# Two attention and gated-MLP layers on one core: block sums by adding transfers in DRAM, and three moves on VectorE and GpSimd

## The chip, the core and the metric

The kernel runs on one core of a Trainium2 chip. A core has TensorE (PE in the profile; its weight loads are PEld), VectorE (DVE), ScalarE (ACT), GpSimd (POOL) and SyncE (SP, which here only issues transfers), 16 DMA engines, an on-chip memory SBUF, and PSUM, eight banks of 128 x 512 float32 that matmuls write into. The metric is the time of one execution on the device in microseconds (us).

## What is computed

Two layers, each a linear-attention block A and then a gated mixer B, both with a residual. All is float32. S = 2048 rows, D = 512, 32 heads of 16, F = 1792 (halves of 896).

```python
x = x + A(layernorm(x));  x = x + B(layernorm(x))      # twice, same weights

def A(x):                       # linear attention
    q, k, v = heads(x @ wqkv)
    phi = lambda t: where(t > 0, t + 1, exp(t)) + 1e-6
    kv = sum_s phi(k)[s] * v[s];  z = sum_s phi(k)[s]
    return (phi(q) @ kv / (phi(q) . z + 1e-6)) @ wo

def B(x):                       # gated mixer
    z = gelu(x @ w_in); z1 = z[:, :896]; z2 = layernorm(z[:, 896:])
    g = w_sp @ z2 + b_sp        # w_sp is 2048 x 2048: it mixes rows
    return (z1 * g) @ w_out
```

## The kernel before

**Split operands.** Every large product is made from two float32r parts of each operand: a high part (a ScalarE copy, `high`, L119) and a low part, the rest (a VectorE subtraction, `low`, L122; for some weights GpSimd's, L127). Three matmuls add up to one product (`mm3`, L133 to L135; `acc`, L902 to L904).

**Order.** The order of instructions on every engine is written out by hand: each engine runs its own in the order of the program and waits on semaphores for the others. SP issues all transfers of before, in program order. Buffers come from rotating lists: 22 pages of 128 x 512 (`pages`, pg), six `quads` (qd) of 2048 columns, four `bigs` (bg), and the eight PSUM banks (`banks`). A buffer's next user waits for its last one.

**P1** (`P1.run`), steps s = 1 to 17, one tile of 128 rows each. A step turns the normalised tile so that its features lie on partitions, splits it (`T_high`, `T_low`), multiplies with the key weights (K), and, up to step ND = 10, with the query weights (Q); the last six query products are put off (`late`, `late_phi`). `Gmm` adds phi(k) transposed times x, two steps behind, in four banks that stay taken. The turning goes through DRAM and a block transpose on VectorE (L260); the first three tiles of the first layer are turned by PE instead. `phi` is ReLU and Exp on ScalarE (L327, L328) and one VectorE operation (L329). `K_split` makes the key's high part (ScalarE, L340) and low part (VectorE, L341), and GpSimd adds the keys up for z (`zacc`, L346). The mixer's second weight `win2` is loaded and split piece by piece in steps 7 to 13 (`side`), loaded a step ahead.

**transition and P2.** `transition` makes the block-diagonal product of the attention, while late query products fill PE. `P2.run`, steps s = 1 to 18: `c` (attention output, added to x by VectorE at L614, then `stats`, L196 to L203, which ends on GpSimd), `b_high` and `b_low` (the next query tile's parts), `a`/`a2` (denominators: GpSimd L561, VectorE L573 to L582), `d` (turned mixer input), `e` (second half of the mixer's input product), `f` (first half). In steps 1 to 4 the remaining late query products (`late`) and their phi (`late_phi`) are woven in.

**P4.** The mixer's 2048 x 2048 product by a fast scheme of seven passes (P2, P1, P6, P7, P4, P5, P3) over 2 x 2 blocks of w_sp. Three passes read blocks of w_sp itself, four read sums of blocks. Then the gates (GpSimd, L929) and the output product `o`.

**Sums.** Class `Sums` makes the four block sums once, in the first layer: a21 + a22 (m = 1), m1 + a11 (m = 2), a21 + a11 (m = 3), m2 + a12 (m = 4), for eight k and two j. A `tick` loads blocks of 128 x 512 into pages, adds them on GpSimd (L782) and stores the sums to DRAM in the next tick (L777). There are 32 ticks with work: four in P1's steps 2 to 5 (on borrowed `bigs`, class `Sheets`), then one in each of P2's steps from 6 on, and P4's first ones. P4 reads each sum tile with one transfer of 512 KB (L831). The second layer reads the same tiles.

Of the kernel before, what the change touches and what calls it, by code (L numbers as in the profile page):

```python
# [52 lines left out]
class Sheets:  # L53


    def __init__(self, slots, n):
        self.slots = slots
        self.tiles = [slots.get([P, NF, 512]) for _ in range(n)]
        self.free_list = deque(t[:, f, :] for t in self.tiles for f in range(NF))

    def get(self, shape):
        return self.free_list.popleft()

    def put(self, *sheets):
        self.free_list.extend(sheets)

    def close(self):
        self.slots.put(*self.tiles)


@with_exitstack
def mixer_kernel(ctx: ExitStack, tc: tile.TileContext, x_in, wqkv, wo_d, win1_d, win2_d, wsp_d, bsp_d, wout_d,
# [40 lines left out]
    def load(ap, slots=pages):  # L113
        t = slots.get(PAGE)
        nc.sync.dma_start(t, ap)
        return t

# [106 lines left out]
    class Turn:  # L224
# [3 lines left out]
        def __init__(self, name, by_pe, always=False):  # L228
            self.name, self.by_pe, self.always = name, by_pe, always
            self.held, self.d, self.raw = {}, {}, {}  # L230
# [20 lines left out]
        def get(self, i):  # L251
# [7 lines left out]
            y = pages.get([P, 4, P])  # L259
            nc.vector.transpose(y.rearrange("p c (t m) -> p m c t", m=4), r.rearrange("p (m c j) -> p m c j", m=4, c=4))  # L260
            pages.put(r)
            return y, pages


    class P1:
        def __init__(self, L):
# [59 lines left out]
        def phi(self, b, r):  # L326
            nc.scalar.activation(r, b, AF.Relu, scale=-1.0)  # L327
            nc.scalar.activation(r, r, AF.Exp, scale=-1.0)  # L328
            nc.vector.scalar_tensor_tensor(r, b, 0.0, r, op0=OP.max, op1=OP.add)  # L329
            banks.put(b)  # L330
# [6 lines left out]
        def K_split(self, i):  # L337
# [3 lines left out]
            nc.vector.scalar_tensor_tensor(l, r, PHI_EPS, h.bitcast(F32), op0=OP.add, op1=OP.subtract)  # L341
            self.pk[i] = (h, l)
            if i == 0:
                self.zacc = r
            else:
                nc.gpsimd.tensor_tensor(self.zacc, self.zacc, r, op=OP.add)  # L346
                pages.put(r)
# [18 lines left out]
        def late_phi(self):  # L366
            if self.later:
                self.Q_phi(self.later.popleft())
# [60 lines left out]
        def run(self, sums):  # L429
            side = deque([self.win2] * NF)  # L430
            ND = NT - DEFER
            for s in range(1, NT + 2):
# [41 lines left out]
                if s > 6 and side:  # L474
                    side.popleft().piece()
                if s > 5 and side:
                    side[0].fetch()


    def transition(p1, p2):  # L480
# [58 lines left out]
        p1.late_phi()  # L539


    class P2:
# [152 lines left out]
        def run(self, sums):  # L695
            w1 = self.win1
            for s in range(1, NT + 3):
                self.loadx(s + 1)
                self.qturn.load(s + 1)
                if s in self.qturn.by_pe:  # L700
                    self.c(s - 1)
                    self.b_high(s)
                    self.c2(s - 1)
                    self.b_low(s)
# [6 lines left out]
                    self.p1.late_phi()  # L711
# [37 lines left out]
                if s > 5:  # L749
                    sums.tick()  # L750
# [6 lines left out]
    class Sums:  # L757

        def __init__(self):
            self.s = {(m, k): dram.tile([P, 2, 512], F32, name=f"s{m}_{k}") for m in range(1, 5) for k in range(HT)}
            self.todo = deque((k, j, h) for k in range(HT) for j in range(2) for h in range(2))
            self.ahead = deque(self.todo)
            self.raw, self.made, self.done = {}, [], []
            self.slots = pages

        def fetch(self):
            if self.ahead:
                k, j, h = self.ahead.popleft()  # L770
                at = ((j, k), (j, k + HT), (2 + j, k)) if h == 0 else ((2 + j, k + HT),)
                self.raw.setdefault((k, j), []).extend(load(wsp_d[n, s], self.slots) for n, s in at)

        def store(self):

            for m, k, j, t in self.made:
                nc.sync.dma_start(self.s[m, k][:, j, :], t)  # L777
            self.slots.put(*self.done)
            self.made, self.done = [], []

        def add(self, m, k, j, t, a, b):
            nc.gpsimd.tensor_tensor(t, a, b, op=OP.add)  # L782
            self.made.append((m, k, j, t))

        def tick(self, ahead=True):
            self.store()
            if not self.todo:
                return
            if not self.raw:
                self.fetch()  # L790
            if ahead or self.todo[0][2] == 0:
                self.fetch()
            k, j, h = self.todo.popleft()
            if h == 0:
                a21, a22, a11 = self.raw[k, j][:3]
                self.add(1, k, j, a22, a21, a22)
                self.add(3, k, j, a21, a21, a11)
                self.done = [a21]
            else:
                _, a22, a11, a12 = self.raw.pop((k, j))  # L800
                self.add(2, k, j, a11, a22, a11)
                self.add(4, k, j, a12, a11, a12)
                self.done = [a22, a11, a12]


    class P4:
# [15 lines left out]
        def fetch(self, g):  # L822
# [7 lines left out]
            else:  # L830
                nc.sync.dma_start(t, self.sums.s[{"P6": 2, "P7": 3, "P5": 1, "P3": 4}[p], k])  # L831
# [172 lines left out]
        def run(self, nxt):  # L1004
# [10 lines left out]
            for g in range(n):  # L1015
# [9 lines left out]
                if g < 16:  # L1025
                    self.sums.tick()
# [88 lines left out]
```

## Time and profile before

| | |
|---|---|
| median of 3 runs | 1404.9 us (1404.71 to 1405.46) |
| the profiled execution | 1404.73 us, of which its span is 1402.9 us |
| PE busy | 1389.6 us, 99% of the span |
| VectorE, ScalarE, GpSimd busy | 886.4, 561.0, 405.6 us |
| DMA | 225.69 MB in 142263 packets, mean 161 GB/s |
| HBM read and written | 156.63 and 67.90 MB |

The span is the time from the first to the last instruction that the profiler recorded; the profiled execution's own time is 1.8 us longer. "Busy" is the time in which an engine runs an instruction; issuing a transfer isn't counted. In rows with an arrow, `out<-in` names the tile written and those read; `[0.65 <-DVE pg L341]` is idle time of the engine ahead of this instruction and what ended it. A row of the waits gives the total, the number and the longest in us. PE's matmuls overlap in the pipeline, so their starts, not their lengths, tell the pace.

### The profile page before, as it was taken

Reading aid. Unit: us, or ns where it says so; the run is one execution under the profiler, and the core shown is the slowest. Engines: PE = TensorE matmul, PEld = TensorE weight load, DVE = VectorE, ACT = ScalarE, POOL = GpSimd, SP = SyncE. Lnnn points to the kernel's source line nnn. Section 1 sums busy time; section 2 is a strip of 40 time slices with the busy share of each in tenths; the row PEclk is TensorE's granted clock in tenths of the full one; section 3 lists DMA queues with packets and bytes.
Section 4 is the critical chain, followed back from the end, with each engine's and each line's share of the span. In section 5 each row is a group of like instructions: output and inputs, shape, how many; then the busy total and the mean of one; then the engine's idle time right before and its main releaser. Section 6 shows DMA issues by size and latency. Waiting matters only on the chain.

```text
span 1402.9 us, 17320 instructions
## 1 busy us (share of the span) xinstructions
PE 1389.6 (99%) x6230; PEld 1156.7 (82%) x6230; DVE 886.4 (63%) x1251; ACT 561.0 (40%) x847; POOL 405.6 (29%) x490
## 2 busy tenths in 40 slices
PE   9999999999999999999999999999999999999998
PEld 7877788888888888888788778888888888888887
DVE  7786777752577666573577867766415466665632
ACT  5564534434323332341356645444333233333420
POOL 4644345544365002040023434432100030022300
PEclk9999999999999999999999999999999999999999
DMA  5842267876897433443635413555334344334432
GB/s 176 270 142 62 73 192 237 271 228 207 305 326 248 134 120 135 173 158 120 210 101 184 129 46 99 179 179 162 114 116 158 104 165 134 133 117 167 155 110 94
DMA packets 142263, 225.69 MB, mean 161 GB/s; under 512 B 11744, under 2 KB 50400, under 8 KB 142176
## 3 DMA queue, kind: packets, MB, share of 16 engines
q1 hardware_dynamic: 142176, 224.57, 48.6%
q8 instruction: 49, 0.80, 0.2%
q14 instruction: 38, 0.31, 0.1%
HBM read 156.63 MB, written 67.90 MB: 160 GB/s over the span
## 4 chain that ended last, share of the span: by engine, by line
PE 87%; DVE 6%; ACT 4%; issue 1%; DMA 1%; POOL 0%; SPq 0%; DVEq 0%; ACTq 0%; POOLq 0%
PE bank L135 15%; PE bank L134 15%; PE bank L133 15%; PE bank L902 13%; PE bank L904 13%; PE bank L903 13%; DVE pg L260 1%; DVE pg L341 1%; DVE pg L329 1%; ACT pg L328 1%; DMA pg<-in_win_dram 1%; ACT pg L327 1%; PE bank L515 1%; PE bank L526 0%; PE bank L221 0%
## 5 line engine op out<-in xcount | busy, mean ns | idle before, releaser
L902 PE MATMUL bank<-qd,pg 128*128 128x512 f32 x800 | 311.2, 389 | 0.0
L904 PE MATMUL bank<-qd,pg 128*128 128x512 f32 x800 | 311.2, 389 | 0.0
L903 PE MATMUL bank<-qd,pg 128*128 128x512 f32 x800 | 311.2, 389 | 0.0
L841 DVE TENSOR_TENSOR qd<-qd,qd 128x1024 fp32r<-128x1024 f32 x112 | 151.8, 1355 | 178.7 <-ACT qd L840 174.2
L840 ACT ACTIVATE qd<-qd 128x1024 fp32r<-128x1024 f32 x112 | 118.5, 1058 | 215.7 <-PE bank L904 199.0
L929 POOL TENSOR_TENSOR bg<-bg,pg 128x512 f32<-128x512 f32 x56 | 85.5, 1564 | 409.7 <-DVE bg L956 195.5
L904 PEld LDWEIGHTS bank<-qd,pg 128*128 128x128 f32 x800 | 150.2, 188 | 31.3
L903 PEld LDWEIGHTS bank<-qd,pg 128*128 128x128 f32 x800 | 150.2, 188 | 31.2
L902 PEld LDWEIGHTS bank<-qd,pg 128*128 128x128 f32 x800 | 150.1, 188 | 31.1
L135 PE MATMUL bank<-qd,pg 128*128 128x512 f32 x384 | 150.7, 392 | 2.5 <-DVE pg L122 2.5
L200 POOL TENSOR_SCALAR rs<-mv 128x1 f32<-128x1 f32 x96 | 36.4, 379 | 384.4 <-DVE mv L198 377.2
L209 ACT ACTIVATE pg<-pg,nb,rs 128x512 f32<-128x512 f32 x63 | 51.1, 811 | 181.6 <-POOL nb L203 175.5
L133 PE MATMUL bank<-qd,pg 128*128 128x512 f32 x288 | 112.4, 390 | 0.0
L134 PE MATMUL bank<-qd,pg 128*128 128x512 f32 x288 | 112.3, 390 | 0.0
L782 POOL TENSOR_TENSOR pg<-pg,pg 128x512 f32<-128x512 f32 x56 | 81.5, 1456 | 47.7 <-DMA pg<-in_wsp_dram 41.8
L133 PE MATMUL bank<-bg,qd 128*128 128x448 f32 x256 | 94.1, 368 | 0.0
L135 PE MATMUL bank<-bg,qd 128*128 128x448 f32 x256 | 93.7, 366 | 0.1
L134 PE MATMUL bank<-bg,qd 128*128 128x448 f32 x256 | 93.6, 366 | 0.0
L135 PEld LDWEIGHTS bank<-qd,pg 128*128 128x128 f32 x384 | 72.0, 188 | 20.8 <-DVE pg L122 6.0
L135 PE MATMUL bank<-wo,qd 128*128 128x512 f32 x224 | 87.3, 390 | 0.8 <-DVE qd L122 0.8
L133 PE MATMUL bank<-wo,qd 128*128 128x512 f32 x224 | 87.3, 390 | 0.7 <-ACT qd L119 0.7
L135 PE MATMUL bank<-qd,bg 128*128 128x512 f32 x224 | 87.4, 390 | 0.0
(121 smaller groups left out, 2571.7 us busy)
## 6 DMA issues: line engine op xcount, KB each, us to landing
qd<-s SPq DMA_DIRECT2D x64, 512.0 KB, 3.4
qd<-in_wsp_dram SPq DMA_DIRECT2D x48, 512.0 KB, 3.8
pg<-x SPq DMA_DIRECT2D x64, 256.0 KB, 2.9
z<-pg SPq DMA_DIRECT2D x56, 256.0 KB, 2.5
pg<-in_wsp_dram SPq DMA_DIRECT2D x56, 256.0 KB, 5.0
s<-pg SPq DMA_DIRECT2D x56, 256.0 KB, 4.8
pg<-z SPq DMA_DIRECT2D x56, 256.0 KB, 5.4
x<-pg SPq DMA_DIRECT2D x48, 256.0 KB, 2.6
```

The source lines that it names most:

```text
L133: nc.tensor.matmul(out, ah, bh, start=start, stop=False)
L134: nc.tensor.matmul(out, ah, bl, start=False, stop=False)
L135: nc.tensor.matmul(out, al, bh, start=False, stop=stop)
L200: nc.gpsimd.tensor_scalar(rs, mv[:, 1:2], LN_EPS, None, op0=OP.add)
L209: nc.scalar.activation(y, x, AF.Identity, bias=nb, scale=rs)
L782: nc.gpsimd.tensor_tensor(t, a, b, op=OP.add)
L840: nc.scalar.activation(w[:, 0], r, AF.Copy)
L841: nc.vector.tensor_sub(w[:, 1], r, w[:, 0].bitcast(F32))
L902: m(out, h[:, o], w[:, 0, j, :], start=start, stop=False, skip_group_check=True)
L903: m(out, h[:, o], w[:, 1, j, :], start=False, stop=False, skip_group_check=True)
L904: m(out, l[:, o], w[:, 0, j, :], start=False, stop=stop, skip_group_check=True)
L929: nc.gpsimd.tensor_tensor(u, u, z1, op=OP.mult)
```

## The change

Four edits, with no change in what is computed and none in the matmuls.

1. **Block sums.** `Sheets`, the loads, the GpSimd adds and the stores are gone. A sum begins as a copy of a block pair (512 KB) from w_sp to DRAM, issued by SP; a transfer issued by GpSimd adds the second operand onto it in DRAM, in rows of 4096 bytes. Eight groups (j, pair of k) start two ticks apart, each spread over six ticks by `PLAN` ("c1" copies for sum 1, "a1" adds to it). Ticks are in P2's steps from 3 on and P4's first eight steps; 20 have work. P4 reads a sum tile in two halves.
2. **Keys' sum.** GpSimd's add to `zacc` gets a dependency on the key's low part, so that it starts behind it.
3. **Turned tiles.** In P1 of both layers, the block transpose writes a PSUM bank instead of a page.
4. **Late query pass and second weight.** The late phi is cut into its ScalarE part (`phi_a`), which stays, and its VectorE part (`phi_b`), which in P2's first steps goes behind the next step's statistics. In P1, the second weight's loads and splits start three steps sooner.

```diff
+    def behind(ins, other):
+        tc.add_manual_dep(ins.ins, other.ins.name, mybir.DependencyInfo(
+            mybir.DependencyClass.Sync, mybir.DependencyReason.DATA))
...
             r = self.raw.pop(i)
-            y = pages.get([P, 4, P])
+            home = banks if self.inbank else pages
+            y = home.get([P, 4, P])
             nc.vector.transpose(y.rearrange("p c (t m) -> p m c t", m=4), r.rearrange(...))
             pages.put(r)
-            return y, pages
+            return y, home
...
-            self.turn = Turn(f"xt{L}", range(3) if L == 0 else ())
+            self.turn = Turn(f"xt{L}", range(3) if L == 0 else (), False, True)
...
+        def phi_a(self, b, r):
             nc.scalar.activation(r, b, AF.Relu, scale=-1.0)
             nc.scalar.activation(r, r, AF.Exp, scale=-1.0)
+
+        def phi_b(self, b, r):
             nc.vector.scalar_tensor_tensor(r, b, 0.0, r, op0=OP.max, op1=OP.add)
             banks.put(b)
...
-            nc.vector.scalar_tensor_tensor(l, r, PHI_EPS, h.bitcast(F32), op0=OP.add, op1=OP.subtract)
+            last = nc.vector.scalar_tensor_tensor(l, r, PHI_EPS, h.bitcast(F32), op0=OP.add, op1=OP.subtract)
...
-                nc.gpsimd.tensor_tensor(self.zacc, self.zacc, r, op=OP.add)
+                behind(nc.gpsimd.tensor_tensor(self.zacc, self.zacc, r, op=OP.add), last)
...
+        def late_phi_a(self):
             if self.later:
-                self.Q_phi(self.later.popleft())
+                self.half = self.qb, ztag(self.later.popleft(), PAGE, f"q{self.L}")
+                self.phi_a(*self.half)
+
+        def late_phi_b(self):
+            if self.half is not None:
+                self.phi_b(*self.half)
+                self.half = None
...
-                if self.L == 0 and s == 2:
-                    sums.slots = Sheets(bigs, 2)
-                if self.L == 0 and 2 <= s < 6:
-                    sums.tick(s < 5)
-                if self.L == 0 and s == 6:
-                    sums.store()
-                    sums.slots.close()
-                    sums.slots = pages
...
-                if s > 6 and side:
+                if s > 3 and side:
                     side.popleft().piece()
-                if s > 5 and side:
+                if s > 2 and side:
                     side[0].fetch()
...
         p2.a2(2)
-        p1.late_phi()
+        p1.late_phi_a()
...
                     self.c2(s - 1)
+                    self.p1.late_phi_b()
                     self.b_low(s)
...
                     self.a2(s + 2)
-                    self.p1.late_phi()
+                    self.p1.late_phi_a()
                     self.a(s + 3)
...
-                if s > 5:
+                if s > 2:
                     sums.tick()
...
+        GROUPS = [(j, k) for k in range(0, HT, 2) for j in range(2)]
+        PLAN = ("c1", "c3"), ("a1", "c2"), ("a3", "c4"), ("a2",), (), ("a4",)
...
+            self.s = {(m, j, k): dram.tile([2, P, 512], F32, name=f"s{m}_{j}_{k}")
+                      for m in range(1, 5) for j, k in self.GROUPS}
+            n, p = len(self.GROUPS), len(self.PLAN)
+            self.todo = deque([(g, x) for g in range(n) if 0 <= t - 2 * g < p for x in self.PLAN[t - 2 * g]]
+                              for t in range(2 * n + p - 2))
...
+        def tick(self):
             if not self.todo:
                 return
+            for g, (what, m) in self.todo.popleft():
+                j, k = self.GROUPS[g]
+                m = int(m)
+                out = self.s[m, j, k]
+                own, k0 = {1: (j, k), 3: (j, k), 2: (2 + j, k), 4: (2 + j, k + HT)}[m]
+                if what == "c":
+                    nc.sync.dma_start(out, wsp_d[own, k0:k0 + 2])
+                else:
+                    n, s = (j, k + HT) if m == 1 else (2 + j, k)
+                    src = wsp_d[n, s:s + 2] if m % 2 else self.s[m // 2, j, k]
+                    nc.gpsimd.dma_start(out, src, accum_op=OP.add, max_dma_last_dim=4096)
...
-                nc.sync.dma_start(t, self.sums.s[{"P6": 2, "P7": 3, "P5": 1, "P3": 4}[p], k])
+                for j in range(2):
+                    nc.sync.dma_start(t[:, j, :], self.sums.tile({"P6": 2, "P7": 3, "P5": 1, "P3": 4}[p], j, k))
...
-                if g < 16:
+                if g < 8:
                     self.sums.tick()
```

More of the change, by code (lines that the diff above doesn't have):

```diff
@@ L50, in put @@
             self.free_list.append(n)
[L53 to L68, printed above, removed]
 @with_exitstack
@@ L366, in late_phi @@
         def late_phi(self):
+            self.late_phi_a()
+            self.late_phi_b()
+        def late_phi_a(self):
             if self.later:
-                self.Q_phi(self.later.popleft())
+                self.half = self.qb, ztag(self.later.popleft(), PAGE, f"q{self.L}")
[3 more added lines that the diff above has]
+                self.phi_b(*self.half)
+                self.half = None
         def xsplit(self, i):
@@ L757, in mixer_kernel @@
     class Sums:
+        GROUPS = [(j, k) for k in range(0, HT, 2) for j in range(2)]
+        PLAN = ("c1", "c3"), ("a1", "c2"), ("a3", "c4"), ("a2",), (), ("a4",)
         def __init__(self):
[L762 to L786, printed above, removed]
+            self.s = {(m, j, k): dram.tile([2, P, 512], F32, name=f"s{m}_{j}_{k}")
[3 more added lines that the diff above has]
+                              for t in range(2 * n + p - 2))
@@ L787, in tick, with tile @@
+        def tile(self, m, j, k):
+            return self.s[m, j, k - k % 2][k % 2]
+        def tick(self):
             if not self.todo:
                 return
[L789 to L803, printed above, removed]
+            for g, (what, m) in self.todo.popleft():
[9 more added lines that the diff above has]
+                    nc.gpsimd.dma_start(out, src, accum_op=OP.add, max_dma_last_dim=4096)
```

6 lines of the change are left out of this document (4 added, 2 removed).

## The prediction

> **What bounds the kernel now.** I read the page's engine lines first, then who TensorE (PE) waited for, then the PE timeline at those waits, then what the other engines did there.
>
> ```profile
> span 1402.9 us, 17320 instructions
> PE 1389.6 (99%) x6230; PEld 1156.7 (82%) x6230; DVE 886.4 (63%) x1251; ACT 561.0 (40%) x847; POOL 405.6 (29%) x490
> PEclk9999999999999999999999999999999999999999
> ```
>
> PE is busy 99% of the span at full clock. The edits take no matmul away, so only the places where PE stands still can give time: 1402.9 - 1389.6 = 13.3 us by this line. All its waits:
>
> ```profile
> PE bank L134 <- DVE pg L341: 3.2, 5, 0.7
> PE bank L135 <- DVE pg L122: 2.5, 4, 0.7
> PE bank L407 <- DVE pg L402: 2.3, 1, 2.3
> PE bank L135 <- DVE qd L122: 0.8, 1, 0.8
> PE bank L133 <- ACT qd L119: 0.7, 1, 0.7
> ```
>
> The first two rows, nine waits with 5.7 us of idle time, are what the edits touch. L407 is the start, and the last two are split output activations and weights at the seam of the two layers; the diff leaves them alone. A wait costs more than its idle time:
>
> ```profile
> 102.26 0.39 PE L135 MATMUL bank<-qd,pg 128*128 128x512 f32 x1
> 102.49 0.39 PE L133 MATMUL bank<-pg,pg 128*128 128x512 f32 x1
> 103.53 0.50 PE L134 MATMUL bank<-pg,pg 128*128 128x512 f32 x1 [0.65 <-DVE pg L341]
> 103.86 0.39 PE L135 MATMUL bank<-pg,pg 128*128 128x512 f32 x1
> ...
> 121.81 0.39 PE L133 MATMUL bank<-pg,pg 128*128 128x512 f32 x1
> 122.28 0.50 PE L134 MATMUL bank<-pg,pg 128*128 128x512 f32 x1
> ...
> 817.21 0.39 PE L133 MATMUL bank<-pg,pg 128*128 128x512 f32 x1
> 817.72 0.50 PE L134 MATMUL bank<-pg,pg 128*128 128x512 f32 x1
> ```
>
> Matmuls start 0.23 us apart (102.26 to 102.49) though each shows 0.39. At the wait the gap is 1.04, and the next one 0.33: lost are 0.81 + 0.10 = 0.91 us where the row shows 0.65 idle, so 0.26 more. Nine waits: 5.7 + 9 x 0.26 = 8.0 us. Two gaps show no idle time at all (121.81 and 817.21): 0.47 and 0.51 instead of 0.23, with the same 0.10 behind: 0.34 + 0.38 = 0.7 us. **8.7 us in all is what these edits can win.**
>
> **Late key steps (five waits and the two gaps).** From step 11 of P1 on, PE does K and G alone, 24 matmuls x 0.227 = 5.4 us a step, instead of 36 or 8.2 us. VectorE's (DVE's) work doesn't shrink that much:
>
> ```profile
> 97.54:104.00 6.46, 5.81 (x26) 4.35 (x25) 5.87 (x9) 4.13 (x7) 3.10 (x4) 1.00 0.52 162
> 74.20:82.40 8.20, 8.20 (x38) 6.80 (x37) 7.22 (x10) 6.04 (x12) 3.24 (x5) 1.00 0.44 133
> L341 DVE SCALAR_TENSOR_TENSOR pg<-pg,pg x32: 691/1601/1773, 18.9 to 820.1; 128x512 fp32r<-128x512 f32 x32
> L346 POOL TENSOR_TENSOR pg<-pg,pg x30: 1291/1662/1676, 24.1 to 819.5; 128x512 f32<-128x512 f32 x30
> L122 DVE TENSOR_TENSOR bg<-pg,bg 128x512 fp32r<-128x512 f32 x14 | 9.5, 682 | 3.9 <-ACT bg L119 3.8
> ```
>
> The first two rows (columns: length, then PE, weight loads, DVE, ACT, POOL busy) are one late step, cut from one transpose to the next, and one full step. In the late step DVE is busy 5.87 of 6.46 us, more than PE's 5.4: DVE sets the pace and PE waits for the key's low part, L341. Two edits cut there.
> - The keys' sum (POOL, L346) runs beside L341 now, and both are stretched: L341 0.69 at its least, where no sum runs, and 1.60 in the middle; L346 1.29 and 1.66. Put behind L341, it leaves 0.91 us a step to DVE. What it meets next in a late step has one operand in SBUF (transpose, statistics, low part from PSUM), so I take no new stretch there; in full steps it meets the weight's low part, at most 0.91 back, where DVE has 8.20 - 7.22 = 1.0 us to spare.
> - The second weight's seven pieces move from steps 7-13 to 4-10: 0.68 us of DVE leave steps 11-13 and enter full steps. There DVE now has 7.22 with L341 stretched and a piece in it already; steps 4-6 become like 7-10, in which PE doesn't wait. The seven fetches go with them on SP's queue; eight block loads and stores of the first layer leave it there.
>
> The late step becomes 5.87 - 0.91 - 0.68 = 4.3 us of DVE under 5.4 of PE. The chain fits as well: from the end of K through two ACT passes, phi, the key's high and low part, five operations at 0.6 to 0.7 or 3.3 us, against the 5.4 us of G and the next K. I count the five waits and both gaps as gone: 3.2 + 5 x 0.26 + 0.7 = 5.2 us.
>
> **Turned tiles in PSUM.** No row shows DVE writing PSUM. The nearest rows:
>
> ```profile
> L260 DVE STREAM_TRANSPOSE pg<-pg 128x512 f32<-128x512 f32 x75 | 80.7, 1077 | 3.9 <-DMA pg<-yt 3.1 <-DMA pg<-xt 0.5 <-issue 0.2
> L122 DVE TENSOR_TENSOR pg<-pg,pg 128x512 fp32r<-128x512 f32 x71 | 54.6, 770 | 13.1 <-ACT pg L119 12.5
> L122 DVE TENSOR_TENSOR pg<-bank,pg 128x512 fp32r<-128x512 f32 x13 | 8.7, 672 | 0.8 <-ACT pg L119 0.7
> ```
>
> Reading PSUM made the low part 0.10 shorter, so I bound the transpose at -0.1 to +1.08 (twice as long) and take 0, the nearest row. Even doubled it leaves a late step at 5.4, equal to PE. The tile takes one of the four banks that G leaves; K's, Q's and this one rotate, and each is next used about a step after its reader ended, so no wait is added.
>
> **Late query pass (four waits).** At the entry of P2, in both layers:
>
> ```profile
> 149.00 0.39 PE L135 MATMUL bank<-qd,pg 128*128 128x512 f32 x1
> 152.64 0.39 PE L134 MATMUL bank<-qd,pg 128*128 128x512 f32 x1
> 153.73 0.50 PE L135 MATMUL bank<-qd,pg 128*128 128x512 f32 x1 [0.70 <-DVE pg L122]
> 150.74 0.58 ACT L119 ACTIVATE pg<-bank 128x512 fp32r<-128x512 f32 x1
> 150.87 0.69 DVE L329 SCALAR_TENSOR_TENSOR z_q<-bank,z_q 128x512 f32<-128x512 f32 x1 [1.91 <-ACT z_q L328]
> 151.48 0.68 DVE L614 TENSOR_TENSOR pg<-pg,bank 128x512 f32<-128x512 f32 x1
> 152.19 0.69 DVE L196 BATCH_NORM_STATS2 st<-pg 128x6 f32<-128x512 f32 x1
> 152.92 0.18 DVE L198 BATCH_NORM_AGGREGATE mv<-st 128x2 f32<-128x6 f32 x1
> 153.01 0.66 DVE L122 TENSOR_TENSOR pg<-bank,pg 128x512 fp32r<-128x512 f32 x1
> ```
>
> DVE stood 1.91 us for ACT's exponential before the query's L329, with L614 behind it, whose matmul ended at 149.4. After the change L614, statistics and aggregate (1.53 us as spaced here) fill that hole, done at 150.95; L329 goes from there to 151.6, and the low part, whose ACT half ended at 151.32, to 152.3. PE wants it at 152.87: 0.6 us early. What is late next is nothing within the step; the second wait a step on is the same picture. The query's bank stays held half a step longer, while eight banks turn and the second product hasn't begun. Gain 2.5 + 4 x 0.26 = 3.5 us.
>
> **Block sums.** Gone: 64 loads and 64 stores of 256 KB on SP and 64 POOL adds. New: 32 copies of 512 KB in DRAM (SP), 32 adding transfers (POOL), over 20 ticks, 16 in P2's steps and four in P4; the sum tiles are then read in halves, 64 more issues. SP's issues fall by 32 net.
>
> ```profile
> 164.00:360.00 196.00, 195.94 (x910) 169.06 (x909) 123.13 (x193) 82.70 (x134) 91.04 (x134) 1.00 0.67 217
> 860.00:1056.00 196.00, 196.00 (x911) 169.65 (x910) 113.94 (x193) 83.58 (x134) 54.50 (x106) 1.00 0.46 150
> 534.00:535.00 1.00, 1.00 (x6) 0.84 (x5) 0.67 (x1) 0.00 (x0) 0.00 (x0) 1.00 1.12 434
> ...
> 254.13 2.66 POOL L782 TENSOR_TENSOR pg<-pg,pg 128x512 f32<-128x512 f32 x2
> 258.97 0.56 POOL L200 TENSOR_SCALAR rs<-mv 128x1 f32<-128x1 f32 x1 [2.19 <-DVE mv L198]
> ```
>
> P2 of the first layer (with sums) and of the second (without) both take 196 us with PE full: today's sums cost nothing, and taking the adds away wins nothing. The question is what replaces them. *POOL:* two adds (2.66 us a step) end 2.2 us before the next statistics; two transfers a step stay within that 4.9 us if one issue costs up to 2.4. No row has a POOL issue: from 0 to, say, an add's 1.33 each; I take 1.33, hidden. Behind it wait the statistics, then ACT's normalising. *DMA:* a P2 step is 196/16 = 12.25 us. The other traffic is 150 GB/s x 12.25 = 1.84 MB; two copies and two adding transfers a step come on top, 1.05 MB of payload each pair. The adding price is in no row: one pass (like a copy) to three (both reads and the write apart). The rate lies between 150/0.46 = 326 and the busiest microsecond's 434 GB/s. Best: 3.94 MB / 434 = 9.1 us. Worst: 6.04 MB / 326 = 18.5. I take two passes at the busiest rate, as queues would be full: 4.99 / 434 = 11.5 us, 94% of the step, so 0 lost. This is the weakest term.
>
> The Trainium skill ("Collectives: The Full Stack", "The bandwidth ceiling: the fold count and why AG ≠ RS ≠ AR") says that a transfer which adds reads two sources and so runs at half a copy's rate; no run here shows it. By it the sum is that of two passes; with it and the lower rate, 326, a step would take 15.3 us and the kernel 3.05 x 14 - 12 = 31 us more, 1427, which is a case of rival 1 below.
>
> **Sum:** 5.2 + 3.5 = 8.7 us off the profiled execution's 1404.73, 1396.0; the median of before lies 0.2 higher. **Prediction 1396.0 us**; own range 1394.5 to 1398.5.
>
> **Rivals.**
> 1. *DMA saturates in the first layer's P2 (slower).* It decides from 12.25 us of DMA a step: with two passes, below 407 GB/s. At three passes and the middle rate of 380: 6.04/380 = 15.9, 3.6 us too many over about 14 full ticks, 51 us, less about one step (12 us), since by the order of the code a turned tile is used a step after it is made: +39, 1435 us; worst (18.5 - 12.25) x 14 - 12 = +75, 1471. For it: both the price and the mixture are unseen, and 94% leaves little. Against it: today's 0.67 moves PE by nothing. Chance 0.26.
> 2. *The saturation just eats the gain*: 1402 to 1407.5, for example two passes at 365 GB/s: 13.7 us a step, 1.42 x 14 - 12 = +8, 1404 us. For and against it stands the same as in 1. Chance 0.08.
> 3. *The late steps don't do what they are meant to*: the sum stretches another DVE operation, or a transpose into PSUM takes twice as long; then only the entry of P2 gains, 1404.7 - 3.5 = 1401.2. For it: POOL and DVE do meet wherever both read SBUF twice. Against it: 1.1 us to spare a step. Chance 0.12, range 1398.5 to 1402.
>
> **Chances.** Forecast 0.54; 0.2% (2.8 us) is about what a measurement of this kernel can tell from no change, so rival 3 also counts as faster: 0.66 faster, 0.08 same, 0.26 slower. Range 1394.5 to 1412: it leaves out 0.02 below and some 0.18 of rival 1.
>
> **What would show it.** Right: L341 near 0.69 in all steps, no PE wait on L341's and L122's successors near 102-122, 150-161, 804-818 and 848-856, PE idle near 5 us. Wrong: a PE wait between 180 and 400, DMA share of P2 near 1, POOL waiting at its transfers, or late steps still 6.4 us apart.

## The result and the profile after

The changed kernel takes 1438.0 us (median of four runs, 1435.9 to 1442.9) against 1405.2 us (1404.7 to 1405.8) for the kernel before on the same chip: ratio 1.0238 [1.0212, 1.0265], slower by 32.8 us. The profiled execution took 1437.4 us. Forecast were 1396.0 us; rival 1, slower in the first layer's P2, is what happened.

Line numbers below are those of the kernel that the fence comes from: 120 to 122 of the changed kernel are the three matmuls that were 133 to 135, 336 is the key's low part (341 before), 248 the block transpose (260), 97 the helper that issues loads (115), and 885 to 887 P4's matmuls (902 to 904). The page of the changed kernel (span, busy time by engine, granted clock in 40 slices, GpSimd's DMA queue, chain that ended last):

```profile
span 1434.8 us, 17177 instructions
PE 1399.5 (98%) x6230; PEld 1165.0 (81%) x6230; DVE 822.0 (57%) x1251; ACT 562.1 (39%) x847; POOL 322.7 (22%) x458
PEclk9999998999999999999999999999999999999999
q0 software_dynamic: 4608, 16.78, 6.7%
PE 80%; DMA 13%; DVE 3%; ACT 1%; issue 1%; POOL 1%; SPq 0%; ACTq 0%; DVEq 0%; POOLq 0%
```

PE does the same 6230 matmuls, now with 35.3 us outside its busy time instead of 13.3, and one of the 40 slices has lost clock. The last row is the news: DMA holds 13% of the chain that ended last. In the kernel before it held 1%:

```profile
PE 87%; DVE 6%; ACT 4%; issue 1%; DMA 1%; POOL 0%; SPq 0%; DVEq 0%; ACTq 0%; POOLq 0%
```

PE's waits of the changed kernel (total, times, longest, in us):

```profile
PE bank L120 <- ACT qd L106: 22.0, 8, 8.9
PE bank L885 <- ACT pg L853: 5.2, 2, 3.8
PE bank L412 <- DVE pg L407: 2.3, 1, 2.3
PE bank L887 <- DVE pg L855: 0.9, 2, 0.6
PE bank L122 <- DVE qd L109: 0.8, 1, 0.8
PE bank L886 <- DVE qd L824: 0.2, 1, 0.2
```

The nine waits that the edits were meant to remove are gone: no row names the key's low part (L336) or the low part of an input tile in a page (L109 into pg). New is the first row, seven of its eight waits, 21.6 us, between 190 and 400 us, up to 8.9 us each: matmuls of P2's products wait for ACT's high part of a turned tile. The windows show where (length, then PE, weight loads, DVE, ACT, POOL busy, granted clock, DMA share, GB/s):

```profile
164.00:360.00 196.00, 174.19 (x769) 146.91 (x768) 101.76 (x174) 68.25 (x111) 70.71 (x120) 0.95 0.92 255
360.00:400.00 40.00, 33.73 (x134) 26.06 (x133) 8.38 (x13) 11.38 (x17) 8.05 (x13) 0.93 1.05 290
213.00:217.00 4.00, 4.00 (x14) 3.57 (x13) 3.80 (x6) 2.66 (x6) 2.19 (x4) 0.57 0.62 164
240.00:251.00 11.00, 4.84 (x13) 4.18 (x14) 4.03 (x6) 3.01 (x5) 1.66 (x4) 0.53 0.78 229
```

In the first layer's P2, DMA went from a share of 0.67 at 217 GB/s to 0.92 at 255, while PE lost 21.8 us of 196 and 5% of its clock. 255 GB/s at 0.92 is 277 GB/s for a full share; I had taken 434. The third row is what follows a wait of 2.2 us, the fourth a wait of 8.9 us and what follows it: in both the clock stands near half.

One such wait, followed through the changed kernel's timeline on SP, DVE, ACT and PE:

```profile
222.17 0.68 SPq L232 DMA_DIRECT2D yt<-pg  x1
241.39 0.32 SPq L97 DMA_DIRECT2D pg<-yt  x1
...
244.36 1.08 DVE L248 STREAM_TRANSPOSE pg<-pg 128x512 f32<-128x512 f32 x1 [7.91 <-DMA pg<-yt]
...
245.48 0.63 ACT L106 ACTIVATE qd<-pg 128x512 fp32r<-128x512 f32 x1 [7.07 <-DVE pg L248]
...
246.16 0.74 PE L120 MATMUL bank<-bg,qd 128*128 128x448 f32 x1 [8.88 <-ACT qd L106]
246.70 0.57 PE L121 MATMUL bank<-bg,qd 128*128 128x448 f32 x1
247.07 0.57 PE L122 MATMUL bank<-bg,qd 128*128 128x448 f32 x1
...
251.24 0.36 PE L122 MATMUL bank<-bg,qd 128*128 128x448 f32 x1
251.44 0.37 PE L120 MATMUL bank<-bg,qd 128*128 128x448 f32 x1
```

SP stores the mixer's tile yt to DRAM at 222.2 and issues the load that brings it back only at 241.4, 19 us later. Load, transpose, high part and matmul then follow in single file. Behind the wait the matmuls start 0.37 us apart until 250.8, then 0.20 apart again, as in the kernel before. That SP stands in between is a row of SP's waits, of the changed kernel and then of the kernel before:

```profile
SPq L97 <- DMA yt<-pg: 108.1, 24, 16.4
```

```profile
SPq L115 <- DMA yt<-pg: 48.1, 24, 2.9
```

SP issues in order and waits for yt's store to land before it issues the reload (and whatever is behind it); the longest such wait grew from 2.9 to 16.4 us. The two rows hold both layers; between 164 and 400 us, in the first, it is 85.0 us in 12 waits, against 24.7 before. The median landing times of the two transfers between 164 and 400 us (12 of each), changed kernel, then before:

```profile
yt<-pg SPq DMA_DIRECT2D x12, 256.0 KB, 7.3
pg<-yt SPq DMA_DIRECT2D x12, 256.0 KB, 5.7
```

```profile
yt<-pg SPq DMA_DIRECT2D x12, 256.0 KB, 2.3
pg<-yt SPq DMA_DIRECT2D x12, 256.0 KB, 2.8
```

**Where the time went.** Against the kernel with the other three edits alone (e1 below, 1395.7) the sums cost 42.3 us. PE's waits between 190 and 400 us are 21.6 + 5.2 + 0.9 + 0.2 = 27.9 us. The 6.3 us of these on L885 to L887 belong to P4's first products, behind a load of w_sp that was issued at 370.1 and took 22.3 us to land; they don't go through yt. The clock comes on top: 196 x 0.05 + 40 x 0.07 = 12.6 us by the mean clock of the first two windows, though PE stands idle in part of the slow time. The pages of the two kernels agree: against e1 (span 1393.0 us, PE busy 1385.5) the changed kernel has 27.8 us more outside PE's busy time and 14.0 us more busy time for the same matmuls, 41.8 together, which is the difference of the spans.

The Trainium skill ("TensorE: Matmul & The Clock Gate", Part 1, "What's actually happening") says that TensorE's clock goes to half after at least one idle window of about 3.4 us. The trace agrees for the wait of 8.9 us (0.53 around it), but the length of a wait alone doesn't tell: one of 2.2 us was followed by 0.57 (213 to 217 us).

### The profile page after: what moved, and what is told of

Its sections match the earlier page's. It is cut to its first block, busy times and chain, and to the rows that moved or that the text cites. A ratio compares the mean times of both kernels' runs of the same rounds, so it can differ in the third digit from the quotient of the medians.

```text
span 1434.8 us, 17177 instructions
## 1 busy us (share of the span) xinstructions
PE 1399.5 (98%) x6230; PEld 1165.0 (81%) x6230; DVE 822.0 (57%) x1251; ACT 562.1 (39%) x847; POOL 322.7 (22%) x458
## 4 chain that ended last, share of the span: by engine, by line
PE 80%; DMA 13%; DVE 3%; ACT 1%; issue 1%; POOL 1%; SPq 0%; ACTq 0%; DVEq 0%; POOLq 0%
PE bank L122 14%; PE bank L120 14%; PE bank L121 14%; PE bank L887 13%; PE bank L885 13%; PE bank L886 13%; DMA yt<-pg 5%; DMA pg<-yt 3%; DMA z<-pg 2%; DMA qd<-in_wsp_dram 2%; DMA pg<-in_wqkv_dram 1%; DVE st L183 1%; PE bank L512 0%; PE bank L523 0%; DVE pg L248 0%
## 5 line engine op out<-in xcount | busy, mean ns | idle before, releaser
L885 PE MATMUL bank<-qd,pg 128*128 128x512 f32 x800 | 312.7, 391 | 5.2 <-ACT pg L853 5.2
L887 PE MATMUL bank<-qd,pg 128*128 128x512 f32 x800 | 312.5, 391 | 0.9 <-DVE pg L855 0.9
L885 PEld LDWEIGHTS bank<-qd,pg 128*128 128x128 f32 x800 | 150.8, 189 | 37.4 <-ACT pg L853 6.0
L887 PEld LDWEIGHTS bank<-qd,pg 128*128 128x128 f32 x800 | 150.8, 189 | 33.1 <-DVE pg L855 1.7
L886 PEld LDWEIGHTS bank<-qd,pg 128*128 128x128 f32 x800 | 150.9, 189 | 32.1 <-DVE qd L824 1.1
L120 PE MATMUL bank<-bg,qd 128*128 128x448 f32 x256 | 97.5, 381 | 21.6 <-ACT qd L106 21.6
L187 POOL TENSOR_SCALAR rs<-mv 128x1 f32<-128x1 f32 x96 | 27.3, 285 | 399.7 <-DVE mv L185 399.0
L122 PE MATMUL bank<-bg,qd 128*128 128x448 f32 x256 | 96.4, 377 | 0.3
L121 PE MATMUL bank<-bg,qd 128*128 128x448 f32 x256 | 96.2, 376 | 0.0
L248 DVE STREAM_TRANSPOSE pg<-pg 128x512 f32<-128x512 f32 x46 | 49.7, 1080 | 68.4 <-DMA pg<-yt 50.8
L122 PE MATMUL bank<-qd,bg 128*128 128x512 f32 x224 | 87.5, 390 | 0.0
L121 PE MATMUL bank<-qd,bg 128*128 128x512 f32 x224 | 87.4, 390 | 0.0
```

The lines of the kernel that those rows point to most:

```text
L120: nc.tensor.matmul(out, ah, bh, start=start, stop=False)
L121: nc.tensor.matmul(out, ah, bl, start=False, stop=False)
L122: nc.tensor.matmul(out, al, bh, start=False, stop=stop)
L187: nc.gpsimd.tensor_scalar(rs, mv[:, 1:2], LN_EPS, None, op0=OP.add)
L885: m(out, h[:, o], w[:, 0, j, :], start=start, stop=False, skip_group_check=True)
L886: m(out, h[:, o], w[:, 1, j, :], start=False, stop=False, skip_group_check=True)
```

## The experiments

The time before was 1405 to 1406 us on every chip used. The theories' letters in the expectations, in short: **S**, the DMA engines saturate: nothing is lost below 12.25 us of DMA a step (the prediction's threshold); **Q**, small packets of SP get too little of each DMA engine beside the new ones, below saturation too; **P**, GpSimd waits at a transfer and its statistics behind it come late; **R** (second series), whatever delays the transfers, it reaches PE only through yt's store, wait and reload.

### The sums and the other three edits apart

**e1_old_sums**, the changed kernel with the block sums of before:

```diff
-                if s > 2:
+                if s > 5:
                     sums.tick()
...
-                nc.gpsimd.dma_start(out, src, accum_op=OP.add, max_dma_last_dim=4096)
...
+                    sums.slots = Sheets(bigs, 2)
```

> The changed kernel with the block sums of before (loads, GpSimd adds, stores) and the other three edits kept. Theory S (in the first layer's P2 the 16 DMA engines have more to do than a step is long: 2 adding transfers x 3.0 us, 96 us of software-queue packets over 32, + 2 copies x 1.4 + other traffic 0.46 x 12.25 = 5.6, together 14.4 us against 12.25) and theory Q (while an adding transfer is on the engines, SyncE's transfers get almost nothing, so each burst delays the store and reload of a turned tile, whatever the total is) and theory P (GpSimd waits for transfers and its statistics come late) all expect 1396 us, no PE wait in the first layer's P2, and the nine waits of before still gone. If one of the other three edits has a part in the loss: above 1402.

Measured 1395.7 us (1394.9 to 1396.2), ratio 0.9929 [0.9915, 0.9944], the forecast's number to 0.3 us. Two rows of its page, then all of PE's waits that are left:

```profile
span 1393.0 us, 17295 instructions
PE 1385.5 (99%) x6230; PEld 1159.2 (83%) x6230; DVE 856.2 (61%) x1251; ACT 561.4 (40%) x847; POOL 386.9 (28%) x490
...
PE bank L430 <- DVE pg L425: 2.3, 1, 2.3
PE bank L138 <- DVE pg L127: 0.8, 1, 0.8
PE bank L140 <- DVE qd L127: 0.6, 1, 0.6
```

**e2_sums_alone**, the kernel before with the new block sums only (the same lines the other way round).

> The kernel before with the block sums as adding transfers, and nothing else of the change. S, Q and P: the loss is that of the sums alone, so 1438 + 8.7 = 1447 us, with PE waits of some 25 to 30 us between 190 and 400 us and the nine old waits back. If the loss came from an interplay with the other edits (earlier weight loads, tiles in PSUM): near 1405.

Measured 1445.1 us (one run), with the old nine waits back and 28.9 us in seven waits for ACT's high part. The loss is the sums' alone, and as far as one run tells the parts add up: 1445.1 - 1405.2 = 39.9 without the other edits, 42.3 with them.

### Which theory: fewer transfers a step, or other ones

**e3_copies_early**: all 32 copies go out in the first layer's P1; only adds are left in P2.

```diff
+                if self.L == 0 and s > 1:
+                    sums.copy()
+                    sums.copy()
...
-        PLAN = ("c1", "c3"), ("a1", "c2"), ("a3", "c4"), ("a2",), (), ("a4",)
+        PLAN = (), ("a1",), ("a3",), ("a2",), (), ("a4",)
...
```

> The changed kernel with all 32 copies issued in the first layer's P1 (two a step in steps 2 to 17); the adding transfers stay where they are. S: a P2 step holds 14.4 - 2.8 = 11.6 us of DMA work, under 12.25, so the stalls go: 1396 to 1402 us. Q: two adding transfers in a row still hold the engines for about 6 us a step: 1415 to 1435, with single PE waits of several us as now. P: GpSimd finds every copy landed and waits for adds alone, 5 us: 1400 to 1410.

1408.2 us, 1.0021 [1.0011, 1.0030]: still 12.5 us above e1, at a DMA share of 0.84 in P2, with 7.1 us of waits on the turned tile. S has no loss there, Q too much.

**e4_spread**: a group each four ticks, and ticks in P1 too (the same line with 4 for 2).

> The changed kernel with a group of sums every four ticks instead of two, and ticks in the first layer's P1 too (34 ticks instead of 20). S: half the sum work a step, 5.6 + 4.4 = 10.0 us of 12.25: no stalls, 1396 to 1398. Q: half as many bursts in P2, mostly one adding transfer at a time: about half the loss, 1410 to 1420. P: 1398 to 1402.

1410.2 us, 1.0035 [1.0023, 1.0046]. P2 is nearly well (PE 194.1 of 196); most of the loss moved into P1, whose late steps are short: 5.5 us of waits for a high part there, and in 100 to 120 us PE busy 16.1 of 20 us at DMA share 0.97.

**e7_every_three**: a group each three ticks, in P2 and twelve steps of P4.

```diff
-            self.todo = deque([(g, x) for g in range(n) if 0 <= t - 2 * g < p for x in self.PLAN[t - 2 * g]]
+            self.todo = deque([(g, x) for g in range(n) if 0 <= t - 3 * g < p for x in self.PLAN[t - 3 * g]]
...
-                if g < 8:
+                if g < 12:
                     self.sums.tick()
```

> The changed kernel with a group of sums every three ticks instead of two, and ticks in P4's first twelve steps; none in P1. A P2 step holds 5.6 + 2/3 x 8.8 = 11.5 us of DMA instead of 14.4. S: under the step of 12.25, so 1396 to 1402. Q: as with the copies moved out (11.6 us, 1408), 1403 to 1410, since bursts of two adding transfers remain in some steps.

1417.4 us, 1.0074 [1.0053, 1.0095]. Above both expectations: at two thirds of the rate, half of the loss stays.

**e5_plain_copies**: GpSimd's transfers as plain copies of the same rows. The second operand overwrites the first, so the addition is left out.

```diff
-                    nc.gpsimd.dma_start(out, src, accum_op=OP.add, max_dma_last_dim=4096)
+                    nc.gpsimd.dma_start(out, src, max_dma_last_dim=4096)
```

> The changed kernel with GpSimd's 32 adding transfers as plain copies of the same rows: the second operand overwrites the first instead of being added to it. Same issues on GpSimd, same bytes landed, no second read. S: a packet of 4096 bytes falls from 327 ns to the 159 ns that such a packet takes elsewhere, a transfer from 3.0 to 1.5 us, a P2 step from 14.4 to 11.4 us of DMA: 1396 to 1402. Q: transfers of SyncE get a third instead of a fifth of an engine beside them (84 ns against 159 or 327) and bursts are half as long: 1400 to 1412. P (the 32 issues on GpSimd of 0.9 to 1.5 us each, and its waits, make the statistics late): nothing changes on GpSimd, so 1430 or more.

1412.4 us, 1.0053 [1.0036, 1.0070]: 25.6 us better, though GpSimd issues the same transfers behind the same waits. P is out: GpSimd's waits for landed transfers between 164 and 400 us are no shorter (25 us, 20 in the changed kernel), and in e9 below, where PE is full, they are 30. GpSimd's queue on this kernel's page (packets, MB, share of 16 engines; the changed kernel's row is above):

```profile
q0 software_dynamic: 4608, 16.78, 3.6%
```

With the spans, 1409.5 and 1434.8 us: 3.6% is 50.7 us for 32 copies, 1.6 us each; 6.7% is 96.1 us for 32 adding transfers, **3.0 us each of all 16 engines**. The records of single packets of 4096 bytes say the same: 159 and 327 ns (medians), a ratio of 2.06. The Trainium skill's rule that I had cited ("Collectives: The Full Stack", "The bandwidth ceiling: the fold count and why AG ≠ RS ≠ AR": two sources read, half the rate) is given there for the reduce step of a ring; the ratio here, 1.9 by the sums and 2.06 by the packets, agrees with it.

**e6_rows_1k**: the adds in rows of 1024 bytes (1024 for 4096 in the same line).

> The changed kernel with the adding transfers cut in rows of 1024 instead of 4096 bytes: four times as many packets, the same bytes. S: the engines have as much to do or more: 1438 or above. Q, in the form that each engine takes one packet from each queue in turn, so that a packet of 84 ns waits for one of 327: the adding packets fall to about 85 ns, SyncE's transfers get half of an engine instead of a fifth, a turned tile's store and reload take a third of the time: 1405 to 1420. P: if an issue on GpSimd grows with the rows: above 1440.

1427.5 us, 1.0141 [1.0124, 1.0158], better by 10.5 us although the queue's packets took 7.7% instead of 6.7%. It lies between S and Q and decides nothing. Its page is that of its slowest run (1434.9 us), in which yt's stores landed in 7.3 us (median), as in the changed kernel; so the trace doesn't show that SP's transfers gain by it.

S, in the form of a threshold for the mean step, is out by e3, e5 and e7: by the prices above their steps need on average some 11.5 to 11.9 us of DMA, under 12.25, and lose 12 to 22 us against e1. But the steps are not alike, which the prediction and the expectations overlook. With groups two ticks apart, `PLAN` gives every other step one copy and three adds, and the steps between three copies and one add. By the same prices that is 16.0 and 12.8 us in the changed kernel, 14.6 and 8.6 in e3, 10.0 to 13.0 in e7. Only e5 stays under 12.25 in every step (11.8 and 11.9, with its copies at 1.5 us), and it still loses 17. What three adds at once do shows in e3, on GpSimd and SP:

```profile
225.58 1.79 POOL L796 DMA_DIRECT2D s<-s  x2
226.76 1.44 POOL L796 DMA_DIRECT2D s<-in_wsp_dram  x1
231.02 0.37 SPq L232 DMA_DIRECT2D yt<-pg  x1
235.75 0.93 POOL L796 DMA_DIRECT2D s<-in_wsp_dram  x1
245.56 0.32 SPq L97 DMA_DIRECT2D pg<-yt  x1
248.67 0.54 SPq L232 DMA_DIRECT2D yt<-pg  x1
254.15 0.32 SPq L97 DMA_DIRECT2D pg<-yt  x1
```

The store at 231.0, issued behind three adds, is followed by its reload 14.5 us later, the next store after 5.5. For the six stores from 231 to 304 us the time to the reload is 14.5, 5.5, 14.3, 5.8, 13.3 and 5.8, and each of e3's three PE waits on a turned tile comes behind a long one. An even plan, two adds in every step, was not run.

Q got the sizes wrong in both directions. So a second series asked which transfers do it and by which way.

### Which transfers, which way to PE

**e10_no_adds**: the copies stay, the adding transfers are left out, so that a sum tile holds its first operand only.

```diff
-                else:
-                    n, s = (j, k + HT) if m == 1 else (2 + j, k)
-                    src = wsp_d[n, s:s + 2] if m % 2 else self.s[m // 2, j, k]
-                    nc.gpsimd.dma_start(out, src, accum_op=OP.add, max_dma_last_dim=4096)
```

> The changed kernel with the adding transfers left out, so that the sum tiles hold their first operand alone; the 32 copies stay on SyncE. A P2 step holds 5.6 + 2.8 = 8.4 us of DMA. S: 1396. R: copies of 512 KB stand ahead of the turned tile's store in SyncE's own queue, three in a row hold it up by 4 us, less than a step of slack: 1396 to 1400. If the copies in that queue are the greater part of the loss: above 1410.

1394.0 us, 0.9913 [0.9896, 0.9929]. Windows of P2 and SP's waits between 164 and 400 us of this kernel:

```profile
164.00:360.00 196.00, 195.43 (x904) 168.14 (x903) 112.57 (x189) 80.52 (x129) 51.11 (x102) 1.00 0.75 238
```

```profile
SPq L97 <- DMA yt<-pg: 70.6, 12, 8.4
```

SP waits up to 8.4 us for yt here, and PE does not notice: so much slack the chain has. With the adds the longest wait is 16.4 us and the total 85.0. So the copies alone bring most of SP's waiting (24.7 us before); what the adds bring is the long waits, and the loss. The time lies just below what S and R expected.

**e8_copies_pool**: the copies are issued by GpSimd too.

```diff
-                    nc.sync.dma_start(out, wsp_d[own, k0:k0 + 2])
+                    nc.gpsimd.dma_start(out, wsp_d[own, k0:k0 + 2], max_dma_last_dim=4096)
```

> The changed kernel with the 32 copies issued by GpSimd too, in rows of 4096 bytes, so that SyncE's queue holds none of the sums' transfers. Same bytes, GpSimd has twice the issues (two more of 1 us a step). S: same work, 1430 to 1445. R: the store no longer stands behind copies in its own queue but shares the engines with more software packets: 1415 to 1435. P (GpSimd): above 1438.

1440.2 us, 1.0252 [1.0219, 1.0284], as the change; SP's longest wait for yt is 20.3 us. Taking the copies out of SP's queue doesn't help, so the loss doesn't need them there. They then go in other packets, beside SP's, so this run doesn't tell what their place in the queue alone was worth.

**e9_no_reload**: all of the first layer's mixer tiles are turned by PE (as the first four are anyway), so that no yt is stored and loaded again in that layer. Its control, **e11_old_sums_no_reload**, is e1 with the same edit.

```diff
-            self.qturn, self.xturn = Turn(f"qt{L}", range(5), True), Turn(f"yt{L}", range(4))
+            self.qturn, self.xturn = Turn(f"qt{L}", range(5), True), Turn(f"yt{L}", range(NT if L == 0 else 4))
```

> The changed kernel with the mixer's input tiles of the first layer all turned by PE (before: the first four), so that P2 of the first layer has no store and reload of a turned tile, on which SyncE waits in order (85 us in 12 waits in the changed kernel, longest 16.4; before 25 and 2.9). 12 x 4 transposes more for PE, 12 stores and 12 loads of 256 KB less. Theory R (the loss comes through that one chain: the store stands behind copies and adding transfers, SyncE waits for it with every later transfer behind it): 1396 plus the transposes' price, 1400 to 1408. Theory S (too much DMA work, whatever its order): the other traffic falls by a quarter, a step from 14.4 to about 13, still over 12.25, and the loads of query tiles and x stay late: 1415 to 1430.

> The control for the run before: the block sums of before, the other three edits, and the first layer's mixer input all turned by PE. 48 transposes of about 0.1 us and the weight switches: 1396 + 5 to 7 = 1401 to 1403. R and S say the same.

1403.9 us, 0.9982 [0.9973, 0.9992], and 1400.7 us, 0.9961 [0.9947, 0.9976]. P2 of e9, then of e11:

```profile
164.00:360.00 196.00, 196.00 (x933) 169.66 (x932) 92.29 (x168) 77.36 (x123) 78.60 (x133) 1.00 0.99 266
```

```profile
164.00:360.00 196.00, 196.00 (x934) 169.86 (x933) 103.48 (x173) 79.81 (x126) 89.93 (x134) 1.00 0.55 182
```

This decides it. With the same sums and a DMA share of 0.99 (e3, e5 and e7 have 0.84 to 0.88), PE is full. The sums cost 1403.93 - 1400.65 = 3.3 us without yt's reload and 42.3 us with it: R holds for nearly all of the loss. The edit also takes 24 transfers away, but by the share the engines are no freer for it. What PE still waits for because of the sums, 4.0 us in e9, is in P4. The turning by PE itself costs 1400.65 - 1395.71 = 4.9 us, so e9 is no gain over e1.

### The three other edits one by one

**s1_behind**: on the kernel before, the keys' sum behind the key's low part, nothing else.

```diff
...
-                nc.gpsimd.tensor_tensor(self.zacc, self.zacc, r, op=OP.add)
+                behind(nc.gpsimd.tensor_tensor(self.zacc, self.zacc, r, op=OP.add), last)
```

> The kernel before with the keys' sum behind the key's low part, nothing else. By the prediction's sum a late step of P1 falls from 5.87 to 4.96 us of VectorE, under PE's 5.4: the five waits on the key's low part and the two gaps go, -5.2 us, 1400. Rival: the sum stretches another VectorE operation instead, the waits stay, 1404 to 1405.

1405.4 us, 0.9999 [0.9989, 1.0008]: nothing. DVE and POOL in one late step of this kernel (start, length; here L346 is the key's low part, L351 the sum, L127 into bg the weight's low part):

```profile
97.24 0.69 DVE L346 SCALAR_TENSOR_TENSOR pg<-pg,pg 128x512 fp32r<-128x512 f32 x1
98.47 1.39 DVE L127 TENSOR_TENSOR bg<-pg,bg 128x512 fp32r<-128x512 f32 x1 [0.53 <-ACT bg L124]
99.79 1.07 DVE L265 STREAM_TRANSPOSE pg<-pg 128x512 f32<-128x512 f32 x1
...
98.02 1.29 POOL L351 TENSOR_TENSOR pg<-pg,pg 128x512 f32<-128x512 f32 x1 [1.46 <-DVE pg L346]
```

The low part is down to 0.69 us, but the sum now meets the weight's low part, which goes from 0.68 to 1.39 with 0.53 us of idle ahead of it. The step is 6.85 us, not shorter (6.46 before). This is rival 3's mechanism. The Trainium skill ("SBUF — State Buffer", "Who interferes with whom") names such pairs, a DVE operation with two SBUF inputs and a GpSimd one that reads SBUF; both pairs here, 0.69 to 1.60 and 0.68 to 1.39, agree.

**s2_weight_early**: the second weight three steps sooner, alone.

```diff
-                if s > 6 and side:
+                if s > 3 and side:
                     side.popleft().piece()
-                if s > 5 and side:
+                if s > 2 and side:
                     side[0].fetch()
```

> The kernel before with the second weight's loads and splits three steps sooner in P1, nothing else. A late step falls from 5.87 to 5.19 us of VectorE against PE's 5.4: the waits on the key's low part go, or all but one or two: -4 to -5.2 us, 1400 to 1401. So either this or the keys' sum would do alone. Rival: the pace is set by the stretched chain, not by the load: 1404 to 1405.

1404.8 us, 0.9994 [0.9985, 1.0004]; L341 still takes 1.60, and its five waits only shrink from 3.2 to 1.4 us, while two waits for an input's high part come in (1.3 us). VectorE's work in a late step is down to 5.2 us, under PE's 5.4, yet its transposes still come 5.9 us apart (95.07, 100.98, 106.91). So the work of VectorE alone doesn't set the pace there; this is the expectation's rival, a chain with the stretched operation in it.

**s3_in_psum**: the transpose into a PSUM bank, alone.

```diff
...
-            self.turn = Turn(f"xt{L}", range(3) if L == 0 else ())
+            self.turn = Turn(f"xt{L}", range(3) if L == 0 else (), False, True)
```

> The kernel before with P1's turned tiles in PSUM, nothing else. The prediction took 0 for it: 1405. The changed kernel's profile shows the transpose at 0.72 us into PSUM against 1.08 into SBUF; by that a late step falls from 5.87 to 5.5 us of VectorE, just over PE's 5.4, and most of the loss on the key's low part goes: 1401 to 1403.

1401.3 us, 0.9970 [0.9959, 0.9981]. Not neutral: it gains 4.3 us. The row of the changed kernel (mean ns of one):

```profile
L248 DVE STREAM_TRANSPOSE bank<-pg 128x512 f32<-128x512 f32 x29 | 20.9, 720 | 0.7 <-DMA pg<-xt 0.7
```

0.72 us into PSUM against 1.08 into SBUF: 0.36 us less DVE in each late step.

**s4_late_pass**: the late query pass cut in two, alone.

```diff
                     self.c2(s - 1)
+                    self.p1.late_phi_b()
                     self.b_low(s)
...
```

> The kernel before with the late query pass behind the statistics, nothing else. The four waits at the entry of P2 go, -3.5 us, 1401.7; the five waits on the key's low part stay. Rival: the low part is late for another reason (ScalarE): 1405.

1401.1 us, 0.9969 [0.9957, 0.9982]; its four waits are gone.

## Why the prediction was wrong

- **Late query pass**, -3.5 us: right, measured -4.4 alone (1405.6 to 1401.1).
- **Late key steps**, -5.2 us: the total with the others came out (e1: 1395.7 for 1396.0), but by which edits isn't shown. The sum meets only "what has one operand in SBUF" in a late step once the weight's pieces have left (s1), and VectorE's work didn't set the pace alone (s2). Alone the two edits give 0.2 and 0.8 us, neither of which can be told from nothing; the pair alone was not run.
- **Turned tiles in PSUM**, taken as 0 with -0.1 to +1.08: outside the bounds, each is 0.36 us shorter. Alone this edit gives 4.3 us, most of what the late steps lost. So it may have covered an error in the line above, and the hit of e1 on the forecast's number is luck as far as that goes. In the changed kernel all late steps have L336 near its least:

```profile
L336 DVE SCALAR_TENSOR_TENSOR pg<-pg,pg 128x512 fp32r<-128x512 f32 x32 | 22.2, 693 | 3.3 <-ACT pg L335 0.3
```

- **GpSimd's issues**, taken as 1.33 us and hidden: the trace has means of 0.97 and 1.10 us, and e5 and e9 show that they are not the trouble.
- **Block sums, the step that failed**: "I take two passes at the busiest rate, as queues would be full: 4.99 / 434 = 11.5 us, 94% of the step, so 0 lost." Two passes were right (3.0 us against 1.6). The rate was not: it came from one microsecond of another mixture of transfers. In engine time a full step is two adds at 3.0, two copies at 1.4 (44.6 us of packets for 32), and the other traffic, 0.46 x 12.25 = 5.6: 14.4 us in a step of 12.25. The 0.46 stood in a row that I had quoted; a sum of shares, not of bytes at a best rate, would have put the likeliest case above the threshold. The "two copies and two adding transfers a step" are a mean as well: the steps take turns at 16.0 and 12.8 us. So the term taken as "0 lost" measured 42.3 us (e1 to the change).
- **The threshold** was wrong as well. Rival 1's formula gives (14.4 - 12.25) x 14 - 12 = +18 us for this step; measured is +42, and kernels with a mean step under the threshold lose 12 to 22, e5 with every step under it 17. I counted a turned tile's step of lead as 12 us of cover. The way is store, wait in SP's order, load, transpose, high part; each transfer on it is slowed long before the mean share is 1 (yt's store lands in 6.8 us at 0.75 in e10, 2.3 before), and PE's clock falls on top. Conversely a share of 0.99 costs PE next to nothing when that way is gone (e9). So rival 1 named the place, and its 1435 us comes near the measured 1438 by luck, from a price too high (three passes) and a way of loss that it lacked.

Open: why yt's store fares so badly. Adding transfers are not needed for that: its median landing is 6.8 us beside the copies alone (e10), 7.3 with the adds. In the trace's packet records the copies go in packets of 32 KB (median 1.25 us), the adds in 4 KB (0.33 us), the stores of turned tiles in 512 bytes (0.03 us), but adds in packets of a quarter of the size gave back only 10.5 us (e6), copies in packets of 4 KB, issued by GpSimd, gave back nothing (e8), and the records do not tell which DMA engine a packet ran on. Nor is it shown how the loss divides between the slower store and reload themselves and SP's wait, which holds up all that is behind it. A reload on another queue, with SP free of the wait, was not tried. e1, with the old sums, is the best version found: 1395.7 us.

## What to carry to other kernels

Where a change adds transfers to a stage, add up engine time per step (the share of before times the step, plus each new transfer by its own packets), not bytes at the best rate seen; then look for a store that the kernel reads back with an in-order wait between, since that is where slower transfers reached PE first here. Look at the fullest step too, not only at the mean. When an operation is moved away from one that it slows, name the next one that it will run beside: alone, such an edit can be worth nothing (s1). Run the parts of a change apart: here three parts won 9.5 us and the fourth lost 42.

## What the runs showed of the hardware that was not expected

- A DVE block transpose of 128x512 f32 takes 0.72 us into PSUM and 1.08 into SBUF.
- An adding transfer of 512 KB within DRAM takes 3.0 us of all 16 DMA engines, a plain copy in the same rows 1.6.
- A 256 KB store that landed in 2.3 us (median) took 6.8 beside plain copies of 512 KB, at a mean DMA share of 0.75 (e10), and 7.3 with adding transfers too, at 0.92.
- A PE wait of some microseconds can be paid twice: behind one of 8.9 us matmuls of 448 columns started 0.37 us apart for 4 us, then 0.20 again; one of 2.2 us was followed by a clock of 0.57 over 4 us.
